# Float32 mixture-of-experts tiles in pairs: seven block products for eight, with the block sums on VectorE

## The chip, the cores and the metric

One core of one Trainium2 chip. The metric is the device time of one execution in microseconds (us); lower is better. A "record" is one matmul instruction as the trace shows it; L848 is line 848 of the kernel that the profile is of.

## The reference

Linear attention over 4 sequences of 768 tokens with 8 heads of 64, then a layer with 8 experts. Each token goes to one expert, either its own best or, where a local gate says so, that of the token before. All data are float32.

```python
h = np.maximum(x[b, s] @ w1[e], 0.0)     # x: 512, w1[e]: 512 x 1024
out[b, s] = p[e] * (h @ w2[e])           # w2[e]: 1024 x 512
```

The change touches only the second part, the experts.

## The kernel before

Tokens are sorted on the chip into tiles of 128 of one expert ("full" tiles) and of 64 ("half" tiles). A tile's rows are gathered by index (GpSimd), turned by TensorE, multiplied with both weight matrices, scaled by the gate, and written to their places by index. The steady loop (cuts marked):

```python
    def hidden(g, half):                       # layer 1, half of it
        ...
        for i in range(FT // 2):
            f = FT // 2 * half + i
            for d in range(DT):
                nc.tensor.matmul(ph[:, i], lhsT=w1t[g % 2][:, d, P * f:P * f + P], rhs=xtt[g % 2][:, d],
                                 start=(d == 0), stop=(d == DT - 1))
        nc.scalar.activation(hts[g][:, FT // 2 * half:FT // 2 * half + FT // 2], ph, ACT.Relu)

    def output(g):                             # layer 2
        ht = hts.pop(g)
        for f in range(FT):
            nc.tensor.matmul(pys[g % 2], lhsT=ht[:, f], rhs=w2t[g % 2][:, f], start=(f == 0), stop=(f == FT - 1))

    def written(g):
        i, j = at(g)
        y = act.tile([P, DM], F32, name="y")
        nc.vector.tensor_scalar(y, pys[g % 2], gate[i][:, j:j + 1], None, ALU.mult)
        nc.gpsimd.indirect_dma_start(out=out, out_offset=bass.IndirectOffsetOnAxis(ap=sidx[i][:, j:j + 1], axis=0),
                                     in_=y, in_offset=None, bounds_check=N - 1, oob_is_err=False)
    ...
        for n in tc.Switch(*halves):           # one arm per number of half tiles
            ...
            for g in range(GA, GB):
                ahead(g + 2)                   # gather of the tile after the next
                hidden(g, 0)
                hidden(g, 1)                   # (half tiles go in between: cut)
                turned(g + 1)
                output(g)
                written(g)
                weights(g + 2)                 # only where the expert changes
```

## Time and profile before

| | before |
|---|---|
| time, median of three runs (range) | 496.55 us (495.72 to 500.88) |
| TensorE busy | 96% of the span, 4231 matmul records |
| VectorE busy | 26% |
| ScalarE busy | 17% |
| moved by DMA | 146.42 MB |

### The profile page before, as it was taken

To read this page: it belongs to the slowest core of one execution; us is meant where nothing else is said; L and a number is where in the kernel's file an instruction comes from. 1 tells how busy PE (TensorE), PEld (TensorE's weight loads), DVE (VectorE), ACT (ScalarE), POOL (GpSimd) and SP (SyncE) were. 2 spreads that over 40 slices of the span, in tenths; PEclk is the share of its full clock that TensorE was granted. 3 is DMA by queue.
4 is the path that set the end of the run, shared out by engine and by line. 5 is a ranking of instruction groups with operands and counts; after the bars stand their busy time and mean duration, and the time that the engine had idled before them with its cause. 6 is when DMAs were issued, how large, how long until landed. Compare 5 with 4: busy or idle time off the path is not lost. (4 is left out here: it accounts for less than half of the span.)

```text
span 493.0 us, 10193 instructions
## 1 busy us (share of the span) xinstructions
PE 475.2 (96%) x4231; PEld 351.6 (71%) x4231; DVE 127.3 (26%) x315; ACT 84.7 (17%) x212; POOL 106.8 (22%) x118
## 2 busy tenths in 40 slices
PE   6999999989999999999999999999999999999992
PEld 5877788776777667658657856876667777666770
DVE  6645677652367301011010101101110110110000
ACT  2256656331110000000000001000000000000000
POOL 5575564300101300221011100201101101110000
PEclk9899999999999999999999999999999999999997
DMA  7999999996788999999999997699954980894000
GB/s 272 411 418 380 352 342 330 401 368 233 260 319 292 324 378 399 395 376 397 398 333 386 398 398 277 211 330 319 327 194 157 310 314 31 284 332 169 23 25 17
DMA packets 49850, 146.42 MB, mean 297 GB/s; under 512 B 3244, under 2 KB 3244, under 8 KB 46960
## 3 DMA queue, kind: packets, MB, share of 16 engines
q1 hardware_dynamic: 42096, 125.86, 69.9%
q0 software_dynamic: 4224, 13.37, 7.1%
q10 hardware_dynamic: 3456, 6.29, 3.4%
q8 instruction: 36, 0.59, 0.5%
q14 instruction: 38, 0.31, 0.2%
HBM read 153.90 MB, written 12.98 MB: 338 GB/s over the span
## 5 line engine op out<-in xcount | busy, mean ns | idle before, releaser
L646 PEld LDWEIGHTS ps<-xt,w 128*128 128x128 f32 x1536 | 175.0, 192 | 14.0 <-issue 12.9
L646 PE MATMUL ps<-xt,w 128*128 128x128 f32 x1536 | 177.1, 276 | 0.8 <-DVE xt L631 0.8
L653 PE MATMUL pk<-w,ht 128*128 128x512 f32 x384 | 168.8, 592 | 0.0
L653 PEld LDWEIGHTS pk<-w,ht 128*128 128x128 f32 x384 | 71.1, 190 | 80.4 <-issue 80.4
L648 ACT ACTIVATE ht<-ps 128x512 f32<-128x512 f32 x48 | 28.7, 598 | 314.7 <-PE ps L646 314.2
L659 POOL DMA_INDIRECT out_dram<-y,sidx x24 | 24.6, 1026 | 196.3 <-DVE y L658 179.3
L658 DVE TENSOR_SCALAR y<-pk,gate 128x512 f32<-128x512 f32 x24 | 18.0, 751 | 146.0 <-PE pk L653 140.6
L637 DVE COPY xt<-po 128x512 f32<-128x512 f32 x23 | 15.9, 691 | 143.2 <-PE po L636 143.1
L621 POOL DMA_INDIRECT xg<-x_dram,gidx x24 | 25.0, 1041 | 121.2 <-PE po L636 84.1
L189 DVE TENSOR_TENSOR sm<-ps,mask 128x512 f32<-128x512 f32 x46 | 29.6, 685 | 15.1 <-PE ps L185 15.0
L165 POOL TENSOR_TENSOR qd<-inp,lamq 128x512 f32<-128x512 f32 x20 | 25.6, 1282 | 23.3 <-PE po L212 8.8
L185 PE MATMUL ps<-inp 64*64 64x128 f32 x736 | 26.3, 282 | 2.0 <-DMA inp<-in_qkv_dram 2.0
L225 PE MATMUL po<-sm,inp 128*64 128x128 f32 x384 | 26.9, 284 | 0.3 <-DMA inp<-in_qkv_dram 0.3
L225 PEld LDWEIGHTS po<-sm,inp 128*64 128x64 f32 x384 | 21.1, 140 | 7.5 <-issue 6.6
L168 POOL TENSOR_TENSOR kd<-inp,rev 128x512 f32<-128x512 f32 x20 | 22.4, 1122 | 16.1 <-PE pk L234 7.6
L185 PEld LDWEIGHTS ps<-inp 64*64 64x64 f32 x736 | 20.6, 136 | 5.6 <-issue 4.6
L246 ACT COPY xn<-pk 128x512 f32<-128x512 f32 x24 | 14.1, 588 | 30.6 <-DMA x_dram<-xn 19.8
L216 ACT ACTIVATE kv<-kv,lamq 128x64 f32<-128x64 f32 x64 | 17.1, 337 | 9.8 <-PE po L212 6.4
L228 ACT COPY xc<-po 128x256 f32<-128x256 f32 x48 | 15.3, 371 | 14.2 <-PE po L225 14.0
L244 PE MATMUL pk<-ident,xc 128*128 128x128 f32 x96 | 15.7, 286 | 0.0
L234 PE MATMUL pk<-inp,kd 128*64 128x64 f32 x320 | 13.2, 222 | 1.2 <-issue 1.1
L636 PE MATMUL po<-ident,xg 128*128 128x128 f32 x92 | 13.8, 273 | 0.0
(182 smaller groups left out, 223.6 us busy)
## 6 DMA issues: line engine op xcount, KB each, us to landing
w<-in_w_dram SPq DMA_DIRECT2D x57, 2048.0 KB
inp<-in_qkv_dram SPq DMA_DIRECT2D x22, 1024.0 KB
x_dram<-xn ACTq DMA_DIRECT2D x24, 256.0 KB
inp<-in_qkv_dram SPq DMA_DIRECT2D x4, 512.0 KB
w<-in_w_dram SPq DMA_DIRECT2D x4, 512.0 KB
xg<-x_dram,gidx POOLq DMA_INDIRECT x24, 7.0
out_dram<-y,sidx POOLq DMA_INDIRECT x24, 6.9
xgh<-x_dram,gidx POOLq DMA_INDIRECT x3, 6.4
```

What stands on the lines that cost most here:

```text
L165: nc.gpsimd.tensor_tensor(qd, x[:, 0].rearrange("p (a i) -> p a i", i=P), lamq, ALU.mult)
L168: nc.gpsimd.tensor_tensor(kd.rearrange("p (h d) -> p h d", d=DH), x[:, 2].rearrange("p (h d) -> p h d", d=DH), rev.unsqueeze(2).broadcast_ ...
L185: nc.tensor.matmul(ps[u][js, a], lhsT=kt[rows, a, js], rhs=qt[rows, a], start=True, stop=True, skip_group_check=True)
L189: nc.vector.tensor_tensor(sm[:, u], ps[u], mask[:, u], ALU.mult)
L216: nc.scalar.mul(kv[:, a], kv[:, a], lamq[:, a, P - 1:P])
L225: nc.tensor.matmul(head(a, u), lhsT=vn[:, a, u], rhs=sm[:, u, a], start=(not c and a < 2), stop=True, skip_group_check=True)
L621: nc.gpsimd.indirect_dma_start(out=xg, out_offset=None, in_=x_dram[:n, :], in_offset=bass.IndirectOffsetOnAxis(ap=gidx[i][:, j:j + 1], axi ...
L646: nc.tensor.matmul(ph[:, i], lhsT=w1t[g % 2][:, d, P * f:P * f + P], rhs=xtt[g % 2][:, d], start=(d == 0), stop=(d == DT - 1))
L648: nc.scalar.activation(hts[g][:, FT // 2 * half:FT // 2 * half + FT // 2], ph, ACT.Relu)
L653: nc.tensor.matmul(pys[g % 2], lhsT=ht[:, f], rhs=w2t[g % 2][:, f], start=(f == 0), stop=(f == FT - 1))
L658: nc.vector.tensor_scalar(y, pys[g % 2], gate[i][:, j:j + 1], None, ALU.mult)
L659: nc.gpsimd.indirect_dma_start(out=out, out_offset=bass.IndirectOffsetOnAxis(ap=sidx[i][:, j:j + 1], axis=0), in_=y, in_offset=None, bound ...
```

## The change

**Intent.** Two tiles of one expert (256 tokens) make a "pair". Each layer of a pair is a product of two 2 x 2 block matrices, done with seven block products in place of eight, at the price of fifteen sums of blocks: four of the weights, four of the tokens' side, seven of results (the last partly by accumulation on TensorE). All block sums go to VectorE, each placed where its result is needed and not earlier. The writes by index are declared free of order among one another. The layout becomes five early tiles as before, then pairs with half tiles between, one pair, single full tiles, and more pairs, with three switches for two.

The core of the diff (cut; the comments are added here):

```diff
+    def sums(out, a, b, c, d, first):
+        sub, tt = ALU.subtract, nc.vector.tensor_tensor
+        if first:
+            return (lambda: tt(out[:, 0], c, d, ALU.add), lambda: tt(c, a, c, sub),
+                    lambda: tt(out[:, 1], out[:, 0], a, sub), lambda: tt(out[:, 2], b, out[:, 1], sub))
+        ...
+    def product_1(to, a, b, new=False):            # one block product of layer 1
+        for m in range(FT // 2):
+            for k in range(2):
+                nc.tensor.matmul(to[:, m], lhsT=a[:, k, P * m:P * m + P], rhs=b[:, k], start=(new and not m and not k),
+                                 stop=(k == 1), skip_group_check=True)
+    def pair(p, hooks={}, next=True, load=True, after=None):
+        ...
+        product_1(a, a1(p, 0, 0), b1(0, 0), True)              # product 1
+        nc.scalar.copy(c01, a)
+        product_1(b, s1[:, 1], xs[:, 1], True)                 # product 2
+        tt(c10, c01, b, ALU.add)                               # line 880
+        sums_2(p, (0, 1))                                      # sums of the layer-2 weights
+        product_1(c, a1(p, 1, 0), b1(0, 1), True)              # product 3
+        product_1(b, s1[:, 0], xs[:, 0])                       # product 4, overwrites what line 880 reads
+        tt(c11, c01, b, ALU.add)
+        tt(c11, c11, c, ALU.add)                               # line 887
+        nc.scalar.activation(h11, c11, ACT.Relu)
+        sums_2(p, (2, 3))
+        product_1(a, a1(p, 0, 1), b1(1, 0))                    # product 5
+        nc.scalar.activation(h00, a, ACT.Relu)
+        product_1(c, a1(p, 1, 1), xs[:, 2])                    # product 6, overwrites what line 887 reads
+        tt(c10, c10, c, ALU.add)
+        nc.scalar.activation(h10, c10, ACT.Relu)
+        product_1(b, s1[:, 2], b1(1, 1))                       # product 7
+        tt(hs[:, 0], h10, h00, ALU.add)
+        tt(hs[:, 1], hs[:, 0], h11, sub)                       # line 900
+        ...
+        product_2(a, h11, b2(p, 0, 0), True)                   # layer 2, product 1
+        ...
+        product_2(b, hs[:, 1], s2[:, 1], True)                 # layer 2, product 2, needs line 900
+        ...                                                    # five more; the next pair's turns and sums between
+    def apart(rows):
+        tc.declare_no_dep(rows.ins, group="out", reason="no row is written twice")
+        tc.add_to_no_dep_group("out", rows.ins)
...
         for n in tc.Switch(*halves):
-            for g in range(GA, GB):
-            ...
+            hooks = hooks_of_halves(n)
+            pair(0, hooks)
+            pair(1, {k - 14: f for k, f in hooks.items()})
+        ...
+        pair(2, ..., load=False)
+        for n in tc.Switch(*fulls):
+            ...                                                # single full tiles
+        pair(3)
+        for k in tc.Switch(*more):
+            last = PMIN + k
+            for p in range(PMIN, last):
+                pair(p, next=p + 1 < last, load=p + 2 < last)
```

The routing that sorts the tokens grows with it (five rows of tables for three, 38 columns for 30).

## The prediction

> **What bounds the kernel now.** I read the page first: engine shares, then the 40 slices.
>
> ```profile
> PE 475.2 (96%) x4231; PEld 351.6 (71%) x4231; DVE 127.3 (26%) x315; ACT 84.7 (17%) x212; POOL 106.8 (22%) x118
> PE   6999999989999999999999999999999999999992
> DVE  6645677652367301011010101101110110110000
> PEclk9899999999999999999999999999999999999997
> DMA  7999999996788999999999997699954980894000
> ```
>
> TensorE is busy in every slice at nearly full clock; from slice 15 on VectorE is nearly idle. A busy matmul row is no proof of a bound, since matmuls overlap, so next the timeline of the steady part (columns: start, duration, engine, line, operation):
>
> ```profile
> 441.09 7.31 PE L646 MATMUL ps<-xt,w 128*128 128x128 f32 x64
> 448.23 0.60 PE L636 MATMUL po<-ident,xg 128*128 128x128 f32 x4
> 448.67 7.03 PE L653 MATMUL pk<-w,ht 128*128 128x512 f32 x16
> 455.54 7.31 PE L646 MATMUL ps<-xt,w 128*128 128x128 f32 x64
> ```
>
> One tile of 128 tokens takes 455.54 - 441.09 = 14.45 us and TensorE starts each piece as it finishes the last. Pieces: layer 1, 64 records; four transposes; layer 2, 16 records. Spacing: (7.31 - 0.28)/63 = 111.6 ns for a 128-wide record, (7.03 - 0.59)/15 = 429 ns for a 512-wide one (0.28 and 0.59 are the durations of single records). Check: 64 x 0.1116 + 0.44 + 16 x 0.429 = 14.45. The view of TensorE's waits adds up to under 10 us, all before 163 us but for 0.8 at 106. So the whole expert stage, 105 to 484 us, is bound by TensorE's streaming: 24 tiles (347 us), three half tiles (288.57 to 310.93 is one tile plus one half: 7.9 us each, 24 us), and small matmuls. The transfers keep up. Only fewer matmuls help here.
>
> **What the Trainium skill says.** (1) "TensorE: Matmul & The Clock Gate", Back-to-back issue gap: a gap is N/2.4 + 2.5 ns when warm; 55.8 for N=128 and 215.8 for 512. The trace shows twice that per record (111.6, 429), two records per float32 product, so the slope holds. I estimate a 256-wide record at half of 429, or 2 x (256/2.4 + 2.5) = 218 ns: I take 216. (2) "VectorE: DVE Perf Modes", the section on the TRN2 errata: a float32 tensor_tensor takes (N+151)/0.96 ns. The trace agrees, with one input in PSUM too: 685 ns for 512 (formula 691), 353 for 192 (357), 419 for 256 (424). So 1024 elements: 1.22 us. (3) "SBUF — State Buffer", Who interferes with whom: a VectorE instruction with two SBUF inputs can block a GpSimd instruction that reads SBUF. Below, the index-driven write beside such an instruction took 1.40 us, not the usual 1.03: it bends GpSimd, not VectorE.
>
> ```profile
> 154.78 0.90 DVE L535 TENSOR_TENSOR hit<-whole,to 128x720 bf16<-128x720 f32 x1
> 155.14 1.40 POOL L659 DMA_INDIRECT out_dram<-y,sidx  x1 [13.58 <-DVE y L658]
> ```
>
> **The change, part by part.** I counted the tokens of the reference's fixed inputs on the host. Before: 24 full tiles, 3 halves. After: 5 early tiles, then 8 pairs (each expert one), 3 full tiles, 3 halves: the same 24 + 3. So the route taken is pairs 0 and 1 (with the halves inside), pair 2, three fulls, pairs 3 to 7.
>
> Gain. A pair does layer 1 in 7 products of 16 records of 128: 112 x 0.1116 = 12.5 us, where two tiles took 128 x 0.1116 = 14.28. Layer 2: 7 products of 8 records of 256: 56 x 0.216 = 12.1, where two tiles took 32 x 0.429 = 13.73. Transposes stay. Saved 1.78 + 1.63 = 3.4 us a pair, pair period about 25.5 us; 8 pairs: **27.4 us**.
>
> VectorE's new work in a pair: eight sums of 1024 (weights of both layers) 8 x 1.22 = 9.8; nine of 512 (four of the hidden rows, five that join products) 9 x 0.69 = 6.2; four of 256 of x, five of 256 with the gate 9 x 0.42 = 3.8. Total 19.8 of 25.5 us, 78%: not the bound by sum, but by order it may be. I laid a pair out by hand, products at 1.79 us (layer 1) and 1.73 (layer 2), a result readable 0.16 us after its product. The tight places: product 6 overwrites what the second c11 sum reads: product 4 readable at 7.3, the two sums end at 8.7, product 6 could start at 8.93: 0.2 us in hand. Layer 2's second product needs hs[1]: the last weight sum ends at 11.15, then c10, ScalarE's relu, two sums: 13.95, wanted at 14.2: 0.25 in hand. All others have over 0.5. So I expect 0 to 0.5 us of stall per pair, 0.2 in the mean: **+1.6 us**. The pairs with halves have more time in them.
>
> Costs outside the pairs. (a) The routing tables have five rows for three, 38 slots for 30. Before, VectorE made them in the gap where TensorE runs tile 2:
>
> ```profile
> 143.46 0.17 DVE L496 TENSOR_SCALAR less<-incl 128x8 f32<-128x8 f32 x1
> 147.83 0.66 DVE L486 TENSOR_TENSOR each<-hot,table 128x288 f32<-128x288 bf16 x1
> 151.38 0.67 DVE L637 COPY xt<-po 128x512 f32<-128x512 f32 x1
> 153.91 7.31 PE L646 MATMUL ps<-xt,w 128*128 128x128 f32 x64
> ```
>
> The copy that tile 3 needs stands behind them and was 1.9 us early (152.05 to 153.91). New: some 6 more instructions of 0.15 us; per half of the tokens 288 to 480 elements in two instructions (+0.4) and three more of 0.17 to 0.2 with their waits (+0.6); one more owner list (+0.6). 0.9 + 2 x 1.05 + 0.6 = 3.6, less 1.9: **+1.8 us** of TensorE waiting. (b) 24 gathering matmuls of 190 columns for 150: +0.4. (c) Before pair 0 the sums of x follow the second transposition directly: copy 0.65, three sums of 0.42, against one product of 1.79: **+0.4**. (d) After pair 2 the first full tile's copy waits for the last gate sum: **+1.3**. (e) Where arms join (pair 2, 3, 4) the gathers wait for scatters of the pair before to land: 1 + 7 us, then the gather's own 1 + 7, wanted at 16 us: 0 to 1 each, **+1.5** in all.
>
> Beside other work: weights are loaded for every pair without condition, since sums overwrite them, 4 MB each 25 us, under the 374 GB/s that the loads of 177 to 311 us reached. During pairs 0 and 1 22 MB are wanted in 75 us, 59 us of that rate: near, but hidden. Scatters without order among them remove waits of GpSimd (13.2 + 10.3 us in its waits), on which TensorE never waited: nothing.
>
> Sum: 496.55 - 27.4 + 1.6 + 1.8 + 0.4 + 0.4 + 1.3 + 1.5 = **476.2 us**.
>
> **The rivals.** *VectorE becomes the bound in a pair.* If 1024-element sums cost more than 1.22 us, or dependent ones drain between them, the two margins go; each 0.1 us on all eight weight sums shifts a chain of four in each layer: about 0.4 us a pair and layer. At 1.0 to 1.5 us a pair: 484 to 488. For: 20 instructions in chains across three engines. Against: the order of instructions is by need, and the formula fits. *Loads become the bound around the halves.* The first half's weights are issued after tile 4's last product and behind 2 MB of pair 1: three loads, 16 us at 374 GB/s, wanted 17 us later. If late: 3 to 6 us, 480. For: the page's DMA digits are 9 there already. Against: fewer loads are open than before. *All is hidden*: none of the small costs shows, 469.
>
> **Range and chances.** The gain is counted from spacings measured over hundreds of records; only the small terms, 7 us, are loose. 469 if they vanish, 486 if VectorE or loads take a further 1.2 us a pair. Faster by over 2% (below 486.6) 0.93, within 2% 0.05, slower 0.02.
>
> **What would show it.** Right: layer-1 and layer-2 records of pairs at 112 and 216 ns; pair starts 25.5 to 25.8 us apart in pairs 4 to 7; VectorE busy 75 to 80% there; its 1024 sums at 1.22 us; tile 3 starting 1 to 3 us late after tile 2's output. Wrong: TensorE waiting over 0.5 us per pair on VectorE's sums or ScalarE's relu, a 256-wide record at much more than 216 ns, or TensorE waiting on a weight load near the halves.

## More of the kernel before

A "call" is one session in which several kernels are timed in turn with the kernel before.

Which arm of a switch runs is decided by numbers that the chip itself has counted; each engine reads the number and branches.

One view adds to what the prediction shows: busy times by stretch, from 340 us to the last tile. Columns: stretch, its length, then busy us and instructions of TensorE, its weight loads, VectorE, ScalarE and GpSimd, then the granted clock, the DMA share and GB/s.

```profile
340.00:441.00 101.00, 101.00 (x589) 74.31 (x588) 10.11 (x14) 8.36 (x14) 14.28 (x14) 1.00 0.70 246
```

In these 101 us TensorE has no gap, VectorE works 10 of them. There is room on VectorE to pay for fewer matmuls.

## The result, and the profile after

474.68 us, median of four runs (473.67 to 476.40), against 496.13 (494.79 to 500.88) in the same rounds: ratio 0.9555, 95% interval 0.9483 to 0.9627. Two later calls on the same kernel gave 0.9603 and 0.9613, both with 475.72 us. A ratio here is the mean time of one kernel's fast runs over that of the other's of the same rounds, so not quite the ratio of the medians. Executions over 1.5% slower than the fastest of the same kernel are left out of the means.

The page of the kernel after: engine totals, then the 40 slices.

```profile
PE 448.6 (95%) x4295; PEld 371.9 (78%) x4295; DVE 263.1 (55%) x507; ACT 108.9 (23%) x260; POOL 110.5 (23%) x118
...
PE   6899979999999899899999999999999999999992
DVE  6743756961339742674464487010186877867750
...
PEclk9999999999999999999999999999999999999997
DMA  7999998995789788999994389980873757560101
```

VectorE went from 127 to 263 us of work and TensorE is still busy in every slice. The slices with a VectorE digit of 0 or 1 about two thirds along are the three single full tiles. The timeline of TensorE in one pair of the steady part:

```profile
364.17 1.95 PE L848 MATMUL ps<-xp,w 128*128 128x128 f32 x16
365.95 1.95 PE L848 MATMUL ps<-xs,s 128*128 128x128 f32 x16
...
373.10 1.95 PE L848 MATMUL po<-xs,w 128*128 128x128 f32 x16
374.88 1.95 PE L848 MATMUL ps<-xp,s 128*128 128x128 f32 x16
376.67 1.89 PE L853 MATMUL pk<-w,h 128*128 128x256 f32 x8
378.40 1.89 PE L853 MATMUL pk<-s,hsum 128*128 128x256 f32 x8
...
389.64 0.61 PE L848 MATMUL ps<-xp,w 128*128 128x128 f32 x4
```

389.64 - 364.17 = 25.47 us for 256 tokens, where two tiles took 2 x 14.45 = 28.90. A layer-1 product takes 365.95 - 364.17 = 1.78 us and a layer-2 product 378.40 - 376.67 = 1.73, as worked out. No line has a wait in brackets (that is, idle time before it and what ended that). VectorE in the same pair (timeline):

```profile
371.51 0.69 DVE L886 TENSOR_TENSOR part<-part,ps 128x512 f32<-128x512 f32 x1 [0.39 <-PE ps L848]
372.23 0.69 DVE L887 TENSOR_TENSOR part<-part,po 128x512 f32<-128x512 f32 x1
...
377.34 0.69 DVE L901 TENSOR_TENSOR hsum<-hsum,h 128x512 f32<-128x512 f32 x1
```

The sum of line 887 ends at 372.23 + 0.69 = 372.92; product 6, which overwrites its input, starts at 373.10: 0.18 us in hand (0.2 predicted). The second sum of hidden rows ends at 378.03 and layer 2's second product starts at 378.40: 0.37 in hand (0.25 predicted). Over four pairs, in the view by stretch:

```profile
338.69:440.58 101.89, 101.89 (x706) 95.71 (x704) 76.48 (x103) 21.35 (x40) 17.12 (x16) 1.00 0.54 186
```

VectorE is busy 76.48 of 101.89 us, 75%, in place of 10%, and TensorE all of it.

Where the two profiled executions part, stage by stage, from the starts of TensorE's groups in the timelines:

| stage | before | after | difference | predicted |
|---|---|---|---|---|
| to the first expert tile (attention) | 106.88 | 108.98 | +2.10 | 0 |
| first tile to tile 3 | 47.03 | 48.09 | +1.06 | +1.8 (a) |
| tile 3 to tile 4 | 16.08 | 16.97 | +0.89 | +0.4 (b) |
| tile 4 to the next stage | 14.53 | 14.97 | +0.44 | 0 |
| from there to the end of the last product | 299.64 | 276.33 | -23.31 | -27.4 + 1.6 + 0.4 (c) + 1.3 (d) + 1.5 (e) = -22.6 |
| to the end | 8.84 | 9.36 | +0.52 | 0 |
| span | 493.0 | 474.7 | -18.3 | -20.4 |

The +0.44 in the fourth row is not term (c): the rows of pair 0's second tile are turned (four records, 0.44 us) before the pair starts, where the kernel before turns only one tile, so the next stage has one such group fewer. Term (c) shows in the next stage: product 2 of pair 0 starts 191.10 - 189.01 = 2.09 us after product 1, 0.30 later than a product takes.

The attention stage is the same code and its length varies from run to run: in the profiles of the changed kernel and its variants the first expert tile starts anywhere from 105.21 to 111.10 us. So 2 us of any single comparison of profiles are chance, and I compare stages, not spans. The profiled execution was the slowest of the four.

Two waits of TensorE in the timeline answer to lines that the prediction showed or to nothing it named. Tile 3 and pair 0:

```profile
157.07 7.41 PE L659 MATMUL ps<-xt,w 128*128 128x128 f32 x64 [1.15 <-DVE xt L652]
...
195.70 0.59 ACT L877 COPY part<-ps 128x512 f32<-128x512 f32 x1 [5.91 <-PE po L848]
196.38 0.69 DVE L880 TENSOR_TENSOR part<-part,ps 128x512 f32<-128x512 f32 x1 [4.21 <-ACT part L877]
197.12 2.05 PE L848 MATMUL ps<-xs,s 128*128 128x128 f32 x16 [2.18 <-DVE part L880]
```

The first is term (a), 1.15 us for 1.8. The others are one chain that I had not foreseen: in the first pair after a switch ScalarE copies the first product only at 195.70, VectorE's sum follows, and product 4 waits 2.18 us for it. Here ScalarE's 5.91 us of idleness are put down to TensorE, but its product was readable at about 190.96. (189.01 is the pair's start; a product takes 1.79 and is readable 0.16 later.) It came late for another reason, which the experiments on the switch look for.

### The profile page after: what moved, and what is told of

Its sections match the earlier page's. It is cut to its first block, busy times and chain, and to the rows that moved or that the text cites. A ratio compares the mean times of both kernels' runs of the same rounds, so it can differ in the third digit from the quotient of the medians.

```text
span 474.7 us, 10504 instructions
## 1 busy us (share of the span) xinstructions
PE 448.6 (95%) x4295; PEld 371.9 (78%) x4295; DVE 263.1 (55%) x507; ACT 108.9 (23%) x260; POOL 110.5 (23%) x118
## 4 chain that ended last, share of the span: by engine, by line
PE 74%; DMA 9%; DVE 9%; issue 4%; ACT 2%; SPq 0%; DVEq 0%; POOL 0%; ACTq 0%; POOLq 0%
PE pk L853 14%; PE ps L848 14%; PE pk L665 10%; PE ps L659 9%; DMA x_dram<-xn 7%; PE pl L853 6%; PE po L848 5%; PE pr L983 2%; PE pr L964 2%; PE po L651 2%; DMA inp<-in_qkv_dram 2%; PE ps L185 2%; PE po L225 2%; DVE sm L189 1%; DVE w L552 1%
## 5 line engine op out<-in xcount | busy, mean ns | idle before, releaser
L659 PEld LDWEIGHTS ps<-xt,w 128*128 128x128 f32 x512 | 58.0, 192 | 6.5 <-issue 3.4
L659 PE MATMUL ps<-xt,w 128*128 128x128 f32 x512 | 59.3, 276 | 3.0 <-DVE xt L652 1.2
L665 PE MATMUL pk<-w,h 128*128 128x512 f32 x128 | 56.3, 592 | 0.0
L848 PE MATMUL ps<-xs,s 128*128 128x128 f32 x256 | 31.5, 276 | 2.4 <-DVE part L880 2.2
L848 PEld LDWEIGHTS ps<-xs,s 128*128 128x128 f32 x256 | 29.9, 192 | 2.9 <-DVE part L880 2.6
L165 POOL TENSOR_TENSOR qd<-inp,lamq 128x512 f32<-128x512 f32 x20 | 25.6, 1280 | 27.3 <-PE po L212 11.6
L848 PEld LDWEIGHTS ps<-xp,w 128*128 128x128 f32 x256 | 30.4, 192 | 1.2 <-issue 0.9
L848 PE MATMUL ps<-xp,w 128*128 128x128 f32 x256 | 31.3, 275 | 0.0
L853 PE MATMUL pk<-w,h 128*128 128x256 f32 x128 | 30.3, 379 | 0.0
L853 PE MATMUL pk<-s,hsum 128*128 128x256 f32 x128 | 30.2, 379 | 0.0
L853 PEld LDWEIGHTS pk<-s,hsum 128*128 128x128 f32 x128 | 24.0, 190 | 3.1
```

Source lines behind the costliest of these rows:

```text
L165: nc.gpsimd.tensor_tensor(qd, x[:, 0].rearrange("p (a i) -> p a i", i=P), lamq, ALU.mult)
L659: nc.tensor.matmul(ph[:, j], lhsT=w1t[w][:, d, P * f:P * f + P], rhs=xtt[i][:, d], start=(d == 0), stop=(d == DT - 1))
L665: nc.tensor.matmul(pys[i], lhsT=hq[f // 4, i][:, f % 4], rhs=w2t[w][:, f], start=(f == 0), stop=(f == FT - 1))
L848: nc.tensor.matmul(to[:, m], lhsT=a[:, k, P * m:P * m + P], rhs=b[:, k], start=(new and not m and not k), stop=(k == 1), skip_group_check= ...
L853: nc.tensor.matmul(to, lhsT=a[:, f], rhs=b[:, f], start=(new and not f), stop=(f == FT // 2 - 1), skip_group_check=True)
```

## The experiments

Twelve runs were made: the changed kernel twice and ten variants. All gave a correct result but the one with six products. "The base" is the changed kernel; edits are against it. Where no base ran in the same call, I compare ratios to the kernel before.

### The base again

> The changed kernel again, unchanged, as the base of this call. Both theories: 473 to 477 us, pairs 3 to 7 starting 25.47 us apart, one wait of about 2.2 us of TensorE in pair 0 if that wait belongs to the program and not to chance. The waits of the attention stage (2.0 us at 64 us in the first profile) should change from run to run, as they come before anything that the change touches.

> The changed kernel unedited, as the base of this call. Both theories: the times of the first two looks again, 472 to 477 us, with the wait of about 2.2 us on the first base sum of pair 0 in the profile.

Measured: 475.72 us both times (472.66 to 477.80 in four runs, 474.88 to 478.06 in six), ratios 0.9603 (0.9523 to 0.9683) and 0.9613 (0.9583 to 0.9643). The waits stand in both profiles: 1.15 us at tile 3; 2.18 and 2.07 us in pair 0; 1.03 and 1.04 us before the full tiles. They belong to the kernel, not to one run.

One thing differs between the executions. In the second profile the granted TensorE clock is 0.57 from 196 to 200 us, just after the wait in pair 0, and pair 0 takes 38.21 us; in the other two profiles of this kernel the clock is 1.00 there and pair 0 takes 36.84 and 36.83. The same dip follows the same wait in the variants with both edits and with one more sum (down to 0.60 to 0.69 over 4 us, pair 0 38.3 to 38.4 us), and not in the other variants. So about 1.4 us of such a difference is no effect of an edit. Why the clock falls after some of these waits and not after others is not shown.

### Is TensorE's streaming the bound? Nine products, and six

```diff
         product_1(b, s1[:, 2], b1(1, 1))
+        product_1(pg.tile([P, A, P], F32, name="po1"), s1[:, 2], b1(1, 1), True)
 ...
+        product_2(pg.tile(..., name="po1").rearrange(...)[:, :D2], h00, s2[:, 2], True)
         product_2(b, hs[:, 3], b2(p, 1, 1))
```

> Two dummy products per pair, one of each layer (16 records of 128 columns, 8 of 256), into a PSUM bank that nobody reads: nine block products of each pair's size are streamed per half instead of seven in one, that is 8 and 8. Theory (TensorE's streaming is the bound and the whole gain is the two products taken away): the pair period goes from 25.47 to 25.47 + 1.79 + 1.73 = 29.0 us, 8 pairs give +28 us, time 500 to 504, slower than the kernel before. Rival (another engine or the loads set the period, TensorE has room): under 10 us more.

505.62 us (505.60 to 505.65, two runs), ratio 1.0205 (1.0119 to 1.0291), some 30 us over the base and 1.6 over the top of what I had expected. Two pair starts, in the timeline of the variant:

```profile
379.62 1.95 PE L848 MATMUL ps<-xp,w 128*128 128x128 f32 x16
...
408.61 1.95 PE L848 MATMUL ps<-xp,w 128*128 128x128 f32 x16
```

A pair now takes 28.99 us, 3.52 more: exactly one product of each layer, 1.79 + 1.73. Eight times 3.52 is 28.2; the rest of the 30 fits the attention stage, where the profiled run lost 2 to 5 us against the base's profiles. So an added product costs its full streaming time.

The other way round, product 7 of layer 1 is left out; the result is wrong (relative error 0.513).

```diff
-        product_1(b, s1[:, 2], b1(1, 1))
```

> The seventh product of layer 1 left out, a wrong result on purpose. By sum VectorE is at 78% and TensorE could go down by 1.79 us a pair. Theory (VectorE's chains from weight sums to hs[1] have only 0.2 to 0.4 us in hand): the second product of layer 2 then waits for hs[1] and the pair gains only 0.3 to 0.5 us: 2.5 to 4 us in all, time 470 to 473, with a wait of about 1.4 us on VectorE ahead of layer 2's second product in each pair. Rival (VectorE follows as long as its share is below 100%): -14 us, about 460.

472.21 us (470.40 to 475.53), ratio 0.9552 (0.9481 to 0.9624), some 3.5 us under the base. The timeline:

```profile
347.69 1.99 PE L853 MATMUL pk<-s,hsum 128*128 128x256 f32 x8 [1.31 <-DVE hsum L900]
...
372.94 1.99 PE L853 MATMUL pk<-s,hsum 128*128 128x256 f32 x8 [1.30 <-DVE hsum L900]
```

The period is 25.25 us: of the 1.79 us taken from TensorE 0.22 are gained per pair and 1.57 given back, 1.30 of them visibly as a wait for VectorE's sum of the hidden rows. Both views are true at once: TensorE sets the time, and VectorE's chain stands a few tenths behind it. By this, TensorE work taken away ahead of the sum of the hidden rows gains little in this order of work (0.22 of 1.79 us); other places were not tried.

### Does "by time of need" matter? The sums of the second layer's weights in one go

```diff
-        sums_2(p, (0, 1))
+        sums_2(p, (0, 1, 2, 3))
 ...
-        sums_2(p, (2, 3))
```

> The four sums of layer 2's weights in one go after the second product, not two and two by time of need; same instructions, same count. Theory: the two c11 sums come 2.5 us later, product 6 waits for them: 2.5 - 0.2 = 2.3 us in each pair without a half tile (6 of them: about 14 us), less in pairs 0 and 1, so +12 to +18 us, time 487 to 493. Rival (order is of no account while VectorE's share is below 80%): within 2 us of the changed kernel.

490.72 us (489.67 to 491.77, two runs), ratio 0.9904, where the base had 0.9603. TensorE's waits from 300 to 470 us in the variant (line waited for, total us, times, longest):

```profile
PE po L848 <- DVE part L887: 8.4, 5, 2.0
```

The same instructions in another order cost 15 us: two sums of 1.22 us now stand ahead of the sums that product 6 waits for, and pairs 4 to 6 take 27.33 to 27.37 us for 25.47. That is about three quarters of the whole gain (by the ratios, 0.9904 for 0.9603).

### How much room is there? One more sum at two places

A useless sum of 512 elements, once ahead of line 887, where 0.18 us were in hand, and once at the end of the pair.

```diff
+        tt(junk, c01, c01, ALU.add)            # e_sum_tight
         tt(c11, c01, b, ALU.add)
 ...
         stt(c01, b, g1, c01, ALU.mult, ALU.add)
+        tt(junk, part[:, 0], part[:, 0], ALU.add)   # e_sum_loose, instead
         scatter(KA + 2 * p + 1, yt[:, 1])
```

> One more sum of 512 elements (0.69 us) on VectorE in each pair, just ahead of the two c11 sums. Theory (0.18 us in hand there by the trace): product 6 starts 0.5 us late in each of pairs 2 to 7, less in pairs 0 and 1, which stretch elsewhere: +3 to +4 us, time 477 to 479. Rival (VectorE has 22% of a pair to spare, 5.6 us, so it is absorbed): 0.

> The same sum of 0.69 us in each pair, but after the last gate sum, where VectorE stood idle for 2.9 us. Both the theory of tight places and the rival: 0 to +0.3 us. If VectorE's total were what counts, it would cost the same as in the tight place.

Tight: 480.02 us (477.18 to 481.53), ratio 0.9715 (the base has 0.9603 and 0.9613 in its calls, so about 1% or 5 us). Loose: 477.67 (476.24 to 480.57), ratio 0.9663 (0.9608 to 0.9718), half of that, and not clear of noise, since the base's intervals overlap this one. In pairs 5 to 7 the periods are 25.54 us (tight) and 25.47 (loose, unchanged). That the tight one costs only 0.07 there, where I had expected 0.5, is explained by the lines of VectorE above: ahead of line 886 it was idle for 0.39 us, which the useless sum fills, and 0.18 were in hand after line 887; 0.68 - 0.39 - 0.18 leaves 0.11. So the total came near the expected 3 to 4 us by luck: the step on which it rested, 0.5 us in each pair, failed, since I had left out the idle time ahead of line 886.

The larger part of both losses lies elsewhere: in the first pair after the last switch, pair 4, which takes 27.2 to 27.3 us in both, and in pair 0, where both profiles have the dip of the clock told above (38.4 and 38.3 us). In the loose one the useless sum also stands ahead of the copy for the first full tile, where TensorE's wait goes from 1.04 to 1.64. The timeline of the loose one, VectorE and TensorE:

```profile
365.40 0.68 DVE L944 TENSOR_TENSOR room<-part 128x512 f32<-128x512 f32 x1
...
370.71 0.69 DVE L881 TENSOR_TENSOR part<-part,ps 128x512 f32<-128x512 f32 x1 [4.64 <-issue]
...
371.45 2.05 PE L849 MATMUL ps<-xs,s 128*128 128x128 f32 x16 [1.39 <-DVE part L881]
```

The chain of what released what shows VectorE branching at 365.15 and its first instruction of the new arm at 370.52. In the base VectorE branches at that place at 364.1 and goes on at 364.7. So entering an arm can cost VectorE 5 us as well. Eleven of the thirteen profiles of this kernel and its variants show 0.5 to 0.6 us at this place; the two that do not are these two (4.8 tight, 5.4 loose), the only builds that add an instruction to each pair's work on VectorE. That points to where the arm lies in VectorE's own instruction stream, but no run tests it.

### Entering an arm

ScalarE in the base, in the chain of waits: start, us, what. L1121 is the branch, L1050 the first instruction of the arm.

```profile
187.47 0.09 ACTq L1121
187.55 5.98 issue
193.53 0.04 ACTq L1050
```

ScalarE does nothing for 5.98 us after its branch. Each engine can be given a hint of where the branch will go, ahead of time (BRANCH_PREFETCH_HINT in the trace). In the base ScalarE's hints for all three switches stand one behind the other, since the scheduler moved them, while TensorE, VectorE and SyncE keep each hint in front of its own switch. So I first put ScalarE's in their written places:

```diff
-    with tc.manual_schedule(engines={PE, DVE, SP}):
+    with tc.manual_schedule(engines={PE, DVE, SP, mybir.EngineType.Activation}):
```

> ScalarE joins the engines whose instructions stay in the written order in the expert part, so its hint for the arm of pairs should stand just before the switch to that arm and not long before, together with two hints for other arms. Theory (ScalarE spends 5 to 6 us fetching the arm's instructions after its branch because its hint came too early and was replaced by later ones): the wait of 2.2 us of TensorE in pair 0 shrinks below 0.5 us, ScalarE's first copy in pair 0 starts within 2 us of its product, and the time falls by about 2 us against the base of this call (0.4%). Rival (those 6 us are the cost of entering any arm, hint or not): the wait stays at 2.0 to 2.3 us and the time stays within 1 us. A third way: the written order of ScalarE is worse somewhere else, and new waits of TensorE on ScalarE rows show where.

475.98 us (473.98 to 476.74), ratio 0.9606 (0.9578 to 0.9635) against 0.9613 for the base of the same call. In ScalarE's instruction order the hints for the second and third switch, which had stood between the first hint and the first branch, now come before their own switches. The same place in the chain of waits:

```profile
187.76 0.06 ACTq L1121
187.82 5.83 issue
193.65 0.04 ACTq L1050
```

The gap is still 5.83 us and TensorE's wait in pair 0 1.90. My theory of the crowded hints has fallen. The base had shown as much: SyncE, whose hints stood in their places all along, branches there at 189.4 and goes on at 195.5, 6.1 us later. What is shown is that the gap begins with the branch and ends with the first instruction of the arm, in every profile of this kernel. What fills it is not. The Trainium skill, "Runtime: NRT & Kernel Launch", Instruction fetch mechanics, says that "a taken branch whose target isn't in the current 2-page window forces a DMA fetch of the target page before execution can continue". The trace agrees that far: packets of an instruction queue appear in such stretches, one of them in the microsecond in which VectorE resumed in the loose variant. From the transfer view of that variant, 370 to 371 us (packets, MB, share):

```profile
q1 hardware_dynamic: 174, 0.36, 98.3%
q14 instruction: 1, 0.01, 2.3%
```

But the record does not name the engine that fetched, and the weight loads (the first line) take nearly all of the engines' time then. That a fetch waits behind them, and that a hint sometimes comes to nothing, is argued and not shown.

### Copies on ScalarE

The two copies that TensorE waited for go from VectorE to ScalarE, which has time there.

```diff
-        turned(1)                              # before tile 3
+        turned(1, copy=nc.scalar.copy)
 ...
-        pair(2, {..., 13: [lambda: turned(0)]}, load=False)
+        pair(2, {..., 13: [lambda: turned(0, copy=nc.scalar.copy)]}, load=False)
```

> The copies of the turned rows of tile 3 and of the first full tile after the pairs go back to ScalarE, which has time there. Theory: they wait on VectorE only because it has the sums and the gathered weights to make at that time; the waits of TensorE of 1.15 us in front of tile 3 and of 1.03 us in front of the fulls shrink below 0.5 us each, and the time falls by 1.2 to 2 us (0.3 to 0.4%). Rival (the product that turns the rows comes too late for any engine): the waits stay above 0.8 us, now on ScalarE, and the time stays within 0.5 us.

477.06 us (471.29 to 479.61; one of the six runs, the 479.61, counts as slow; the median of the five fast ones is 476.99), ratio of the fast ones 0.9579 (0.9532 to 0.9626), which cannot be told from the base's 0.9613. Two of the runs, 471.29 and 472.63, lie below all six of the base; the profile is of a run of 477.63. The wait at tile 3 is gone, that before the full tiles went from 1.04 to 0.72. But in the timeline, one step later:

```profile
164.60 1.58 PE L562 MATMUL pr<-w,lane 128*128 128x190 bf16 x17 [1.62 <-DVE w L552]
```

The matmuls that gather the routing tables waited 0.21 us for VectorE in the base; now they wait 1.62. Tile 3 no longer waits, but the tables that VectorE makes next are not ready sooner: VectorE itself is the bound between tiles 2 and 4, and the copy was only one piece of its work. The copy's 0.59 us on VectorE are not even freed: in the chain of waits VectorE now spends 0.55 us there on reading the number of the arm (DVEq L1027), which had run beside the copy, and line 682 follows line 517 by 9.54 us in both. Neither theory as I had put it was right: ScalarE did take the copy in time, and the stage from the first expert tile to pair 0 takes 80.02 us as in the base's first look.

This profile also shows a wait that the base's profiles do not have, in pair 3:

```profile
356.07 0.66 PE L651 MATMUL po<-ident,xg 128*128 128x128 f32 x4 [1.88 <-DMA xg<-x_dram,gidx]
```

A gather, issued after GpSimd had waited for a write of the tile before to land, came 1.9 us late. Against the base's second look it was issued only 0.2 us later after the pair's start; but it landed 7.8 us after its issue, for 3.5. That is the prediction's term (e), in one execution and not in another, and it costs this profile 2.1 us that the two fastest runs need not have lost: what the copies are worth without it is not shown.

> Both edits in one kernel. Theory: the gains add, 3 to 4 us under the base of this call (0.7 to 0.8%), some 471 us, with no wait of TensorE over 0.6 us between the first expert tile and the end. Rival of either edit: only the other one's share remains, or nothing.

That expectation failed. Both edits together: 475.55 us (473.31 to 477.07), ratio 0.9601 (0.9570 to 0.9631), the same as the base. The waits are 1.64 us at the tables and 2.24 in pair 0. There is no version here that beats the changed kernel.

### First-layer weights of the pairs loaded twice

```diff
             weights_of(KA + 2 * p + 4, w_of(p), (1,))
+            weights_of(KA + 2 * p + 4, w_of(p), (1,))
```

> The first layer's weights of the pairs loaded twice: 6 times 2 MB more, which brings the traffic from 126 to 138 MB, near the 146 MB of the kernel before. Theory (loads are hidden): within 1 us of the changed kernel, at most a wait near the half tiles. Rival (a part of the gain is the 21 MB that are no longer loaded): +4 to +12 us.

488.45 us (487.45 to 489.31), ratio 0.9879: 13 us slower, not "within 1 us". TensorE waited 2.85 us for the first half tile's weights of pair 1 and 10.47 us at the start of pair 2, which together are the 13 us; from pair 3 on it waited for no load. The waits of SyncE's queue between 180 and 300 us in this variant:

```profile
SPq L624 <- DMA w<-in_w_dram: 32.9, 4, 13.2
```

The base has 4.1 to 4.4 us in that row. The second load writes the same buffer, so it waits for the first to land, and every later load behind it in SyncE's queue waits too. The edit was thus a test of the queue's order more than of the rate: it shows that in pairs 0 to 2 the loads have less than 13 us to spare, and that the later pairs have room for a delay of that kind. How near the rate itself is stays open.

### Writes in order

```diff
-        tc.declare_no_dep(rows.ins, group="out", reason="no row is written twice")
-        tc.add_to_no_dep_group("out", rows.ins)
+        pass
```

> The declaration that scatters need no order among them taken out, so that each scatter waits for the one before to land. Theory (TensorE never waits on them): within 1 us. Rival (in the pairs, where two scatters follow each other within 2.5 us and gathers queue behind them on GpSimd, a gather comes late for the transposes): +0.5 to +2 us per pair, 4 to 16 us.

484.24 us (483.46 to 486.19), ratio 0.9785: about 8.5 us slower than the base, where I had said that the declaration is worth nothing. GpSimd's timeline around the start of pair 2 (269.26 here):

```profile
277.75 0.98 POOL L673 DMA_INDIRECT out_dram<-y,sidx  x1 [7.08 <-DVE part L885]
281.15 1.05 POOL L636 DMA_INDIRECT xg<-x_dram,gidx  x1 [2.41 <-DMA out_dram<-y,sidx]
```

And in the base, where pair 2 starts at 267.58:

```profile
269.30 0.98 POOL L674 DMA_INDIRECT out_dram<-y,sidx  x1 [1.49 <-issue]
275.81 1.04 POOL L636 DMA_INDIRECT xg<-x_dram,gidx  x1 [5.53 <-DMA out_dram<-y,sidx]
```

The second write of the pair goes out 8.49 us after the pair's start for 1.72, since it waits for the first to land (the view names VectorE's line 885, but the rows of this write were ready at 270.20, and the first write, issued at 269.49, took 7.4 us to land), and the gather behind it 11.89 us after for 8.23. TensorE, which needs the gathered rows, then waits (timeline of the ordered variant):

```profile
288.64 0.63 PE L651 MATMUL po<-ident,xg 128*128 128x128 f32 x4 [2.98 <-DMA xg<-x_dram,gidx]
```

A second such wait of 1.93 us stands in pair 3; as the unordered variant with ScalarE's copies shows one of 1.88 there, it need not be due to the order. At the very end the last write waits for the one before:

```profile
476.55 0.98 POOL L673 DMA_INDIRECT out_dram<-y,sidx  x1 [2.99 <-DMA out_dram<-y,sidx]
```

It is issued 3.97 us after the write before it; in the base 2.22. From the last pair's start to the end of the span it is 35.8 us for the base's 33.9. So the declaration is worth the 3.0 us in pair 2 with some 1.7 more around it (pair 2 to the full tiles took 32.24 us; 27.51 and 27.53 in the base's two profiles; the granted clock in the 6 us from that wait on was 0.72, and 28% of 6 us are these 1.7), 1.8 at the end, and at most 2 in pair 3: 6.5 to 8.5 us, which covers what was timed.

## Why the prediction was right, and where its steps failed

The time (474.68, later 475.72 us for a predicted 476.2) and the mechanism were right; the sum of the small terms came out right in part because errors in it cancelled.

- **The gain, 27.4 us: right.** Pairs 3 to 6 take 25.47 us; 8 x (28.90 - 25.47) = 27.4. The extrapolated 216 ns of a 256-wide record holds: a group of eight takes 1.73 us, eight times 0.216. The nine-product variant puts the same price on a product from the other side.
- **VectorE's sums: right.** A sum of 1024 takes 1.22 to 1.23 us and one of 512 0.68 to 0.69. VectorE is busy 75% in the pairs, for 78% worked out. The two margins were 0.18 and 0.37 us for 0.2 and 0.25.
- **"0 to 0.5 us of stall per pair, 0.2 in the mean: +1.6 us": wrong in place, right in size.** Pairs 3 to 7 have no wait at all. But one pair lost 2.1 to 2.2 us, pair 0, and pair 2 0.2 in the first profile: because ScalarE and VectorE resumed late after a branch. The prediction laid no time against entering an arm. I took "pairs with halves have more time in them" as a reason that nothing would happen there; the wait is in the first two products, before any half tile.
- **(a) the tables, +1.8: 1.15 as a wait, and it is a VectorE bound, not a late copy.** I named the copy as what tile 3 would wait for, and it is; but taking it off VectorE moved the wait to the tables. (Its sum was 3.6 - 1.9 = 1.7, not 1.8.) (b) +0.4 for the wider gathering matmuls: 0.4 in the matmuls (2.17 us for 1.77), and they start 0.5 later, of which 0.2 shows as a wait. (c): 0.3 for 0.4. (d): 1.0 for 1.3, but not for the reason given: with the copy on ScalarE, where no gate sum stands ahead of it, 0.72 stays, so most of it is the way from turning the rows to the copy.
- **(e) joins, +1.5: 0 in the three profiles of the kernel itself, 1.9 once in a variant with the declaration.** The mechanism is there, the size is a matter of how soon a transfer lands in that execution.
- **"Scatters without order remove waits of GpSimd on which TensorE never waited: nothing": failed.** The argument read GpSimd's waits in the kernel before and saw that no TensorE wait followed. But the changed kernel writes two tiles within 2.5 us of each other at the end of a pair and gathers for the next pair behind them. There the order would cost 6.5 to 8.5 us. The step judged a dependence in the old layout, while it only bites in the new one. The total was not hurt, since the changed kernel has the declaration; the net is the same, but its value was not seen.
- **Point (3), the write of 1.40 us for 1.03 beside a VectorE instruction with two SBUF inputs:** not borne out as the cause. In pairs 3 to 6 of the changed kernel the first write by index at the end runs beside VectorE's sums of x, which have two such inputs, and takes 0.99 to 1.04 us. Nothing in the sum rested on it.
- **The rivals.** "VectorE becomes the bound" is refuted for the kernel as it is, and confirmed as near: two sums in the wrong place cost 15 us. "Loads become the bound around the halves" did not happen, though the doubled loads show that place to be the only one where TensorE then waits for weights.

**Left open.** What fills the 6 us after ScalarE's branch; why VectorE enters the same arm in 0.5 to 0.6 us in eleven profiles and in 4.8 and 5.4 in two; why the clock falls after some waits; and how near the load rate is in pairs 0 and 1. About 0.9 us of the last stage's difference is not assigned to a line.

## What to carry to other kernels

Where TensorE streams without waits and VectorE is idle, block products with fewer multiplications were worth their streaming time here (3.43 us a pair), with each sum placed just ahead of its use: two of the same sums, two products earlier, gave back three quarters of the gain. Once the margins are a few tenths of a microsecond, look at the seams (the first pass after a branch, the end of the program, index-driven writes that wait for each other), not at the steady loop. And before moving work off the engine that a wait names, ask whether that engine's next result is due as well: the wait may just move one instruction on. And when two profiles differ by a microsecond or two, look at the granted clock after each wait before giving the difference to an edit.

## What the Trainium skill lacked or had wrong

- "Runtime: NRT & Kernel Launch", Instruction fetch mechanics, names the stall after a taken branch but gives it no size and does not speak of hints. Here ScalarE stood still for 5.83 to 5.98 us between a branch with a hint and its first instruction of the arm, VectorE for 0.6 us in the same kernel and 5.4 in a variant.
- "TensorE: Matmul & The Clock Gate", Back-to-back issue gap, gives no time for float32. Here a float32 matmul of the kernel shows two records, each spaced at about twice the page's N/2.4 + 2.5: 111.6 ns for 128, 216 for 256, 429 for 512. The section's sustained figures, about 81 ns for N = 128 and 131 ns for N = 512, do not fit these records even when doubled (162 and 262).
- "VectorE: DVE Perf Modes", The TRN2 errata: (N+151)/0.96 for a float32 tensor_tensor, confirmed there at 512 and 2048, holds at 1024 too: 1.22 us measured, 1.224 by formula, also with an in-place output. The fused multiply and add with a gate per row took 0.48 us for 256 elements, where the formula for the plain sum gives 0.42.
- I found no page that says what order between index-driven writes costs. Here the second of two ordered writes waits for the first to land and its issue slips from 1.72 to 8.49 us after the pair's start.
